# A decode kernel of two interleaved attention and feed-forward layers: all of its order tables exchanged for another set

## The chip, the cores and the metric

One core of one Trainium2 chip runs the whole program. The metric is the device time in microseconds; lower is better. The program before was timed three times.

## The reference

Four batch rows x (4 x 1 x 512) go through attention, a gated feed-forward block, the same attention and the same feed-forward block again, each with a residual:

```python
def _A_ref(x, k_cache, v_cache, wq, wo):          # k, v: 4 x 8 x 4096 x 128, bfloat16
    q = (x @ wq).reshape(B, Sq, 32, 128).transpose(0, 2, 1, 3)
    k = jnp.repeat(k_cache, 4, axis=1); v = jnp.repeat(v_cache, 4, axis=1)
    p = softmax(einsum("bhqd,bhkd->bhqk", q, k) * 128 ** -0.5)
    return einsum("bhqk,bhkd->bhqd", p, v).transpose(0, 2, 1, 3).reshape(B, Sq, 4096) @ wo
def _B_ref(x, w_gate, w_up, w_down):              # 512 x 1792, 512 x 1792, 1792 x 512
    return (sigmoid(x @ w_gate) * (x @ w_up)) @ w_down

x = x + _A_ref(layernorm(x), k_cache, v_cache, wq, wo)
x = x + _B_ref(layernorm(x), w_gate, w_up, w_down)
x = x + _A_ref(layernorm(x), k_cache, v_cache, wq, wo)
x = x + _B_ref(layernorm(x), w_gate, w_up, w_down)
```

Both layers read the same caches: 4 batches x 8 heads x (K and V) of 1 MB each, 64 MB in one layer.

## The kernel before

**Units and pairs.** A unit is one layer, one batch and one key-value head; there are 2 x 4 x 8 = 64, numbered in the order in which they run. Two neighbouring heads make a pair; the 32 pairs are numbered g = 0 to 31, and `ORDER` lists them as (layer, batch, pair of heads). Unit i belongs to pair i // 2.

**Slots.** A K or V tile of a unit fills one slot. There are 12, and when the last batch's second query product is done, the four tiles of the query weights WQ become four more (`wq_done`). `RET` names the tiles that stay in their slots from layer 0 to layer 1, 30 in all; these are loaded once, the others twice. A K slot comes free behind the last `scores` that reads it, a V slot behind the last `pv`. `LOADS` is the order of all loads on SyncE's queue: `k` and `v` are the next unit's K and V, `o` is the next tile of the output weights WO (which one, by `WO_ORDER`), `s` the next of the six halves of the gate, up and down weights (WG, WU, WD). `pump()` is called after each instruction that frees a slot, and issues loads in this order until one needs a slot and none is free. SyncE runs in order, so a load that waits for its slot holds up all behind it.

**Steps.** Step k carries the scores and softmax of pair k and the PV product of pair k - 1, unless `EARLY` lets a pair's PV run in its own step. Within a step:

- `k_turn` transposes a K tile in place on VectorE (L1164), whole or in two halves; `scores` are the products of the query with K (L1180); `smax`, `spread_max`, `softmax` find the maximum, spread it over the rows (L1240) and take the exponentials with their sum on ScalarE (L1265); `ptrans` turns the weights (L1310), and 16 small copies, shared between ScalarE (L1344) and VectorE (L1338) by `SHARE`, lay them out; `pv` multiplies with V (L1414). `PV_WIDE` repeats the columns of the moving operand to 32, 48 or 64 of which four are used. `normalise` (L1505) divides by the sums.
- `wo_mm` projects a pair's output, and where two batches or layers meet it does both at once. By `WO_ROW` it runs in column form (32 products, L1566) or in row form (16 products L1536, a copy on ScalarE L1545, four turning products L1549). `WO_AT` gives its place in the step.
- `STEP` codes four choices per step: where the next pair's K tiles are transposed (`turn_at`, `late`), whether in halves (`cut`), whether `pv` stands ahead of `spread_max` (`pv_first`), and whether a pair's two `pv` stand together (above 71). `FIRST_AT` gives the place at which the next pair's first scores are issued.
- `FILL` puts products of the identity with itself (L1199, `fill`), whose result nobody reads, on TensorE's queue at a place of a step.

```python
turn_at, pv_first, cut, late = STEP[k] % 3, STEP[k] // 3 % 2, STEP[k] // 6 % 4, STEP[k] // 24 % 3
...
pv_both, pv_late = both and STEP[k] > 71 and pv_first, both and STEP[k] > 71 and not pv_first
```

**Between the layers.** When a batch has all eight heads of layer 0, 23 pieces (`pass_steps`) carry it through the feed-forward block and the query of layer 1: `ln_a` (sums, L752), `wide` (up and gate products, L973), the inverse root by Newton steps on VectorE, `up_copy`, `gate_mul` (L996, L1001), `h_turn` (L1016), `down` (L1087), `down_add` (L1109), `ln_a` again, `q_row` (L1034), `q_out`, `q_turn`, `q_spread` (L878). `PLACES` gives each piece a step and a place. Batches 0, 1, 2 and 3 do so in this order.

**The start and the end.** The WO rows are loaded in pairs and put in order by `wo_turn` (L636, and copies L646 and L651) at the places of `WO_TURN`. The last pair's V comes in quarters (`v_parts`), its products (`pv_last`, L1441) interleave with its output projection (L1775) and with sums that give the mean (L1797, prepared by `wo_sum` at the places of `WSUM`). `AHEAD` places the first three batches' layer norm for the last feed-forward block; that block then runs for all four batches (L920, L2018) and writes the output.

**Order.** All engines run their instructions in program order; waits between engines are semaphores. Each table only moves instructions or chooses a form; none changes the result's arithmetic beyond order.

Of the kernel before, what the change touches and what calls it, by code (L numbers as in the profile page):

```python
# [20 lines left out]

ORDER = [
    (0, 0, (0,)),
    (0, 0, (3,)),
    (0, 0, (2,)),
    (0, 1, (1,)),
    (0, 0, (1,)),
    (0, 2, (0,)),
    (0, 1, (0,)),
    (1, 0, (1,)),  # L30
    (1, 0, (2,)),
    (0, 1, (3,)),
    (0, 1, (2,)),
    (1, 0, (3,)),
    (1, 0, (0,)),
    (0, 2, (2,)),
# [6 lines left out]
    (0, 3, (3,)),  # L43
    (1, 2, (3,)),
    (0, 3, (0,)),
    (0, 3, (2,)),
    (0, 3, (1,)),
    (1, 2, (1,)),
    (1, 2, (0,)),
    (1, 2, (2,)),  # L50
# [5 lines left out]

PLACES = [
    (
# [4 lines left out]
    ),  # L63
    (
# [4 lines left out]
    ),  # L69
    (  # L70
# [4 lines left out]
    ),  # L75
    (
# [4 lines left out]
    ),  # L81
]


FIRST_AT = (
# [4 lines left out]
)  # L90

LOADS = (
    "kooookokovkvkkvokokvvvkksvvkksvvksskkssk",
    "vvvkkvkvkkvvkkvkvkvkvvkvkvkvkvkvkvvkvvkk",
    "kkkvvvvkkvkvkvvkkvvkkvkkvvkvvkkkvvvkvkkv",
    "kvvvkkvkvvkkkvkkvvvvvv",
)


SHARE = (  # L100
# [4 lines left out]
)  # L105


WO_AT = (
# [4 lines left out]
)  # L113


WO_ROW = (
# [4 lines left out]
)  # L121


EARLY = (
# [4 lines left out]
)  # L129


WO_ORDER = (1, 3, 7, 2, 4, 0, 6, 5)

WO_TURN = (
# [4 lines left out]
)  # L139


PV_WIDE = (
# [4 lines left out]
)  # L147


FILL = {  # L150
# [3 lines left out]
}  # L154


WSUM = (
    (7, 8), (28, 0), (22, 5), (18, 7),
    (22, 0), (29, 7), (27, 4), (29, 7),
)  # L160


AHEAD = ((29, 2), (30, 8), (32, 4))


STEP = (
# [5 lines left out]
)  # L172


# [136 lines left out]
def bass_interleave_layers__gqa_block_cached__glu_gated_glu__decode_kernel(  # L311
# [154 lines left out]
    for kinds in LOADS:  # L466
        for kind in kinds:
            if kind == "o":
                loads.append(("wo", WO_ORDER[got["o"]]))
            elif kind == "s":  # L470
# [155 lines left out]
    def wo_turn(m, ps, key):  # L626
        assert not row_live[0]
        n, a = WO_ORDER[m // 2], m % 2
        assert f"wo{n}" in S.last_write
# [1502 lines left out]
```

## Time and profile before

| | |
|---|---|
| time, median of 3 runs | 304.89 us (302.9 to 305.69) |
| profiled execution: span, first to last instruction | 306.1 us; the page gives no other time of this execution |
| mean granted TensorE clock | 0.883 |
| busy: TensorE / VectorE / ScalarE / GpSimdE | 224.3 / 205.7 / 131.2 / 26.0 us |
| read from HBM | 116.66 MB |

In a row of the windows view stand the stretch, its length, the busy time of PE, PEld, DVE, ACT and POOL with their instruction counts, the granted TensorE clock, the DMA share and GB/s. In a timeline row stand the start, the length, the engine, the line, the operation, its output and inputs, the shape and the count; in brackets the idle time before it and what ended that.

### The profile page before, as it was taken

Reading aid. Unit: us, or ns where it says so; the run is one execution under the profiler, and the core shown is the slowest. Engines: PE = TensorE matmul, PEld = TensorE weight load, DVE = VectorE, ACT = ScalarE, POOL = GpSimd, SP = SyncE. Lnnn points to the kernel's source line nnn. Section 1 sums busy time; section 2 is a strip of 40 time slices with the busy share of each in tenths; the row PEclk is TensorE's granted clock in tenths of the full one; section 3 lists DMA queues with packets and bytes.
Section 4 is the critical chain, followed back from the end, with each engine's and each line's share of the span. In section 5 each row is a group of like instructions: output and inputs, shape, how many; then the busy total and the mean of one; then the engine's idle time right before and its main releaser. Section 6 shows DMA issues by size and latency. Waiting matters only on the chain.

```text
span 306.1 us, 11460 instructions
## 1 busy us (share of the span) xinstructions
PE 224.3 (73%) x4993; PEld 157.6 (51%) x4993; DVE 205.7 (67%) x600; ACT 131.2 (43%) x521; POOL 26.0 (9%) x107
## 2 busy tenths in 40 slices
PE   0384386864687888688886777888868688987886
PEld 0331043543464466566554554665546456556676
DVE  4755677885766368875854997566788668357743
ACT  1031243552205246564451874627772443646310
POOL 0000000000000010000001110001000000012200
PEclk9999999999579897979999857589788979599977
DMA  7999999999999979999999999999999999999900
GB/s 283 420 397 415 422 414 416 418 418 421 418 416 403 388 295 418 423 415 416 388 394 378 415 422 421 419 418 422 420 416 418 413 412 415 400 345 411 377 18 3
DMA packets 20094, 117.40 MB, mean 384 GB/s; under 512 B 1992, under 2 KB 1996, under 8 KB 7500
## 3 DMA queue, kind: packets, MB, share of 16 engines
q1 hardware_dynamic: 20044, 116.67, 93.9%
q8 instruction: 39, 0.64, 0.8%
q14 instruction: 11, 0.09, 0.1%
HBM read 116.66 MB, written 0.00 MB: 381 GB/s over the span
## 4 chain that ended last, share of the span: by engine, by line
DMA 45%; PE 30%; DVE 12%; SPq 5%; ACT 4%; issue 3%; POOL 0%; POOLq 0%; DVEq 0%; ACTq 0%
DMA slot<-in_A_v_cache_dram 22%; DMA slot<-in_A_k_cache_dram 12%; PE O_ps L1414 9%; DMA wd<-in_B_w_down_dram 6%; DVE slot L1164 6%; DMA wo<-in_A_wo_dram 5%; PE S_ps L1180 5%; ACT pT L1344 2%; SPq L550 2%; SPq L528 2%; PE M_ps L636 2%; PE O_ps L1566 2%; PE M_ps L1034 1%; PE M_ps L1087 1%; DVE wo L651 1%
## 5 line engine op out<-in xcount | busy, mean ns | idle before, releaser
L1164 DVE STREAM_TRANSPOSE slot<-slot 128x1024 f32<-128x1024 f32 (+1 forms) x61 | 100.9, 1663 | 7.0 <-DMA slot<-in_A_k_cache_dram 6.9
L1344 ACT ACTIVATE pT<-PT 32x64 bf16<-32x64 f32 x392 | 84.3, 215 | 31.9 <-PE PT L1310 26.9
L1414 PE MATMUL O_ps<-pT,slot 128*128 128x32 bf16 (+2 forms) x1888 | 65.8, 190 | 16.2 <-DMA slot<-in_A_v_cache_dram 9.6
L1414 PEld LDWEIGHTS O_ps<-pT,slot 128*128 128x128 bf16 x1888 | 59.6, 101 | 23.3 <-DMA slot<-in_A_v_cache_dram 10.6
L1180 PE MATMUL S_ps<-slot,qz 128*32 128x256 bf16 x1008 | 48.9, 329 | 12.5 <-DVE slot L1164 7.2
L1265 ACT ACTIVATE pe<-S_ps,small 128x256 bf16<-128x256 f32 x32 | 15.2, 474 | 63.3 <-DVE small L1253 63.2
L1180 PEld LDWEIGHTS S_ps<-slot,qz 128*32 128x32 bf16 x1008 | 25.3, 107 | 24.8 <-DVE slot L1164 9.2
L1279 POOL TENSOR_TENSOR small<-small 128x1 f32<-128x1 f32 x64 | 12.4, 193 | 217.6 <-ACT pe L1265 215.1
L646 ACT ACTIVATE wo<-M_ps 128x512 bf16<-128x512 f32 x14 | 8.3, 595 | 35.0 <-PE M_ps L636 35.0
L1338 DVE CAST pT<-PT 32x64 bf16<-32x64 f32 x88 | 19.4, 221 | 5.6 <-PE PT L1310 4.1
L1566 PE MATMUL O_ps<-oT,wo 128*128 128x32 bf16 x576 | 19.7, 188 | 1.1 <-issue 0.5
L636 PE MATMUL M_ps<-wo,row 64*128 64x512 bf16 x56 | 13.3, 565 | 9.1 <-DVE wo L651 5.5
L1566 PEld LDWEIGHTS O_ps<-oT,wo 128*128 128x128 bf16 x576 | 18.2, 101 | 2.1 <-DVE oT L1505 1.1
L1217 DVE TENSOR_REDUCE small<-S_ps 128x1 f32<-128x256 f32 x32 | 13.2, 413 | 8.0 <-PE S_ps L1180 7.8
L903 POOL TENSOR_TENSOR qz<-qc,norm 128x128 bf16<-128x128 bf16 x32 | 12.6, 399 | 45.5 <-ACT qc L889 45.5
L1240 PE MATMUL MS<-row_max,mask_f 128*128 128x16 bf16 x64 | 6.6, 176 | 13.1 <-DVE row_max L1223 12.6
L651 DVE CAST wo<-M_ps 128x512 bf16<-128x512 f32 x14 | 9.5, 680 | 9.6 <-PE M_ps L636 9.5
L1505 DVE TENSOR_TENSOR oT<-O_ps,rden 128x8 bf16<-128x8 f32 x31 | 4.9, 159 | 14.4 <-PE O_ps L1414 9.8
L1240 PEld LDWEIGHTS MS<-row_max,mask_f 128*128 128x128 bf16 x64 | 4.3, 107 | 19.2 <-DVE row_max L1223 17.7
L1199 PE MATMUL MS<-ident_bf 128*128 128x256 bf16 x69 | 12.2, 316 | 0.4
L1310 PE MATMUL PT<-ident_bf,pe 128*128 128x128 bf16 x64 | 10.0, 245 | 2.9 <-ACT pe L1265 2.6
L1253 DVE CUSTOM_DVE_ANT_0 row_max<-MS,small 128x16 bf16<-128x16 f32 x32 | 7.0, 217 | 7.3 <-PE MS L1240 7.1
(143 smaller groups left out, 231.1 us busy)
## 6 DMA issues: line engine op xcount, KB each, us to landing
slot<-in_A_v_cache_dram SPq DMA_DIRECT2D x49, 1024.0 KB, 12.5
slot<-in_A_k_cache_dram SPq DMA_DIRECT2D x43, 1024.0 KB, 11.3
wq<-in_A_wq_dram SPq DMA_DIRECT2D x4, 1024.0 KB, 7.8
wo<-in_A_wo_dram SPq DMA_DIRECT2D x8, 512.0 KB, 15.8
wq<-in_A_v_cache_dram SPq DMA_DIRECT2D x3, 1024.0 KB, 12.3
slot<-in_A_v_cache_dram SPq DMA_DIRECT2D x8, 256.0 KB, 13.6
wg<-in_B_w_gate_dram SPq DMA_DIRECT2D x2, 896.0 KB, 18.9
wu<-in_B_w_up_dram SPq DMA_DIRECT2D x2, 896.0 KB, 16.2
```

Source lines behind the costliest of these rows:

```text
L636: (lambda h, i, rows: lambda e: e.matmul(ps[h][:, :], lhsT=spread_w[i][rows, :], rhs=wo_sb[rows, c + i, :], start=(i == 0), stop=(i == 1), ...
L651: lambda e: e.tensor_copy(wo_sb[:, c + 1, :], ps[1][:, :]),
L903: lambda e: e.tensor_tensor(qz_sb[z][:, :, 0:4 * REP].rearrange("p i (a r) -> p i a r", r=REP), qc_sb[:, b, u:u + 2, :, :].rearrange("p u ...
L1164: dve(lambda e: e.transpose(kf, kf), writes=[f"s{st}"])
L1180: (lambda t, b2, e_, w0, s: lambda e: e.matmul(S_ps[p][32 * s:32 * s + 8 * REP, 0:2 * P], lhsT=qzf[:, w0:w0 + 8 * REP], rhs=ktv[:, :, s, : ...
L1217: lambda e: e.tensor_reduce(m, S_ps[p][:, 0:2 * P], AX.X, ALU.max),
L1265: lambda e: e.activation(to, frm, ACTF.Exp, bias=nm_sb[p], scale=exp_scale, accum_out=sm_sb[p][0],),
L1279: (lambda n: lambda e: e.tensor_tensor(sm_sb[p][n + 1], sm_sb[p][n], top(sm_sb[p][n]), ALU.subtract))(n),
L1338: (lambda dst, frm: lambda e: e.tensor_copy(dst, frm))(dst, frm),
L1344: (lambda dst, frm: lambda e: e.activation(dst, frm, ACTF.Copy))(dst, frm),
L1414: (lambda x, c, j: lambda e: e.matmul(O_ps[p][:, ul * OW:ul * OW + PV_WIDE[g]].rearrange("p (w n) -> p w n", n=REP), lhsT=vv[:, x * JG + c ...
L1566: (lambda c, r: lambda e: e.matmul(wide_out(O_ps[p], OWO + c, nb), lhsT=wo_sb[:, u * REP + r, bass.ds(2 * P * (c // 2) + c % 2, P, step=2) ...
```

## The change

Fifteen tables get other values; no line of the code and no entry of `RET` changes, so 30 tiles stay held. The new values come from a search that judges each choice by twenty runs of a model in which random waits are doubled.

- `ORDER` changes within pairs 1 to 10 and swaps pairs 23 and 24; `LOADS`, `WO_ORDER`, `WO_TURN` follow another order of loads.
- `FILL` goes from 16 places and 69 products that run (the entry at (33, 1) is never read) to 10 places and 89 products: 24 at step 5 in place of 19, none in step 6 in place of 12, 14 in step 11, 18 in step 17, and 11, 8 and 12 at the end of steps 24 and 25 and at the start of step 26.
- `WO_ROW` has 7 pairs in row form in place of 9, pair 30 among them now; `EARLY` 2 pairs in place of 4; 13 pairs have 64 PV columns in place of 9, the last pair among them.
- `PLACES`, `STEP`, `FIRST_AT`, `WO_AT`, `SHARE`, `WSUM` and `AHEAD` move the pieces of the steps. `STEP` of the last step codes the same end of the program as before.

```diff
@@ -21,16 +21,16 @@
 
 ORDER = [
     (0, 0, (0,)),
+    (0, 0, (2,)),
     (0, 0, (3,)),
-    (0, 0, (2,)),
+    (0, 2, (0,)),
+    (0, 0, (1,)),
     (0, 1, (1,)),
-    (0, 0, (1,)),
-    (0, 2, (0,)),
     (0, 1, (0,)),
+    (1, 0, (2,)),
     (1, 0, (1,)),
-    (1, 0, (2,)),
+    (0, 1, (2,)),
     (0, 1, (3,)),
-    (0, 1, (2,)),
     (1, 0, (3,)),
     (1, 0, (0,)),
     (0, 2, (2,)),
@@ -43,8 +43,8 @@
     (0, 3, (3,)),
     (1, 2, (3,)),
     (0, 3, (0,)),
+    (0, 3, (1,)),
     (0, 3, (2,)),
-    (0, 3, (1,)),
     (1, 2, (1,)),
     (1, 2, (0,)),
     (1, 2, (2,)),
@@ -56,119 +56,115 @@
 
 PLACES = [
     (
-        (2, 2), (2, 3), (2, 3), (2, 3), (2, 4), (2, 4),
-        (2, 4), (2, 4), (2, 4), (3, 2), (3, 3), (3, 4),
-        (3, 5), (3, 5), (3, 5), (3, 5), (3, 5), (3, 5),
-        (3, 5), (3, 5), (3, 5), (3, 6), (3, 6),
+        (2, 3), (2, 4), (2, 4), (2, 5), (2, 5), (2, 5), (2, 5), (2, 6), (2, 6),
+        (2, 8), (2, 8), (3, 0), (3, 1), (3, 2), (3, 2), (3, 2), (3, 2), (3, 2),
+        (3, 4), (3, 5), (3, 5), (3, 6), (3, 6),
     ),
     (
-        (2, 1), (2, 2), (2, 2), (2, 2), (2, 5), (2, 5),
-        (2, 5), (2, 5), (2, 5), (3, 1), (3, 1), (3, 2),
-        (3, 4), (3, 6), (3, 6), (3, 6), (3, 7), (3, 7),
+        (2, 1), (2, 2), (2, 2), (2, 3), (2, 4), (2, 4), (2, 6), (2, 6), (2, 6),
+        (3, 0), (3, 0), (3, 2), (3, 4), (3, 6), (3, 6), (3, 6), (3, 7), (3, 7),
         (3, 7), (3, 7), (3, 7), (3, 8), (3, 8),
     ),
     (
-        (1, 8), (2, 0), (2, 0), (2, 1), (2, 2), (2, 2),
-        (2, 2), (2, 2), (2, 2), (2, 3), (2, 4), (2, 6),
-        (2, 7), (3, 0), (3, 1), (3, 1), (3, 1), (3, 1),
-        (3, 1), (3, 2), (3, 2), (3, 6), (3, 6),
+        (1, 8), (2, 1), (2, 1), (2, 1), (2, 1), (2, 1), (2, 2), (2, 2), (2, 2),
+        (2, 5), (2, 5), (2, 6), (3, 0), (3, 0), (3, 0), (3, 1), (3, 1), (3, 1),
+        (3, 2), (3, 2), (3, 5), (3, 6), (3, 6),
     ),
     (
-        (1, 8), (2, 1), (2, 1), (2, 1), (2, 1), (2, 1),
-        (2, 2), (2, 2), (2, 2), (2, 3), (2, 4), (2, 6),
-        (2, 8), (3, 1), (3, 2), (3, 3), (3, 3), (3, 5),
-        (3, 5), (3, 5), (3, 5), (3, 6), (3, 6),
+        (1, 8), (2, 1), (2, 1), (2, 1), (2, 1), (2, 1), (2, 1), (2, 1), (2, 2),
+        (2, 3), (2, 3), (2, 6), (2, 8), (2, 8), (2, 8), (2, 8), (2, 8), (2, 8),
+        (3, 1), (3, 4), (3, 4), (3, 5), (3, 5),
     ),
 ]
 
 
 FIRST_AT = (
-    7, 7, 6, 7, 5, 6, 1, 3,
-    8, 7, 1, 3, 1, 0, 4, 8,
-    2, 7, 5, 2, 7, 1, 7, 7,
-    0, 5, 2, 7, 8, 8, 3,
+    6, 8, 8, 2, 4, 7, 6, 1,
+    5, 2, 0, 6, 1, 8, 8, 5,
+    7, 2, 4, 2, 7, 1, 8, 7,
+    0, 3, 7, 4, 2, 1, 6,
 )
 
 LOADS = (
-    "kooookokovkvkkvokokvvvkksvvkksvvksskkssk",
-    "vvvkkvkvkkvvkkvkvkvkvvkvkvkvkvkvkvvkvvkk",
-    "kkkvvvvkkvkvkvvkkvvkkvkkvvkvvkkkvvvkvkkv",
-    "kvvvkkvkvvkkkvkkvvvvvv",
+    "kookoookkkvokkvvkovovkvvkvksvkvksssskksk",
+    "vvkvvkvkkvkkvkkvvkvkvvkkvkvvkvkvvkkvvkkv",
+    "vkkvkkkvvvvkvvkvkkvvkvkkkkkvvvvkkvkvvkkk",
+    "vkvvvvkkkvvkkvvvkkvvvv",
 )
 
 
 SHARE = (
-    1, 0, 1, 2, 2, 0, 2, 1,
-    0, 0, 1, 0, 1, 2, 0, 0,
-    0, 0, 0, 0, 0, 1, 0, 2,
-    1, 0, 0, 2, 1, 6, 2,
+    1, 0, 1, 0, 1, 0, 0, 1,
+    0, 1, 0, 1, 1, 2, 0, 0,
+    0, 1, 0, 1, 0, 1, 0, 1,
+    1, 0, 0, 1, 1, 6, 2,
 )
 
 
 WO_AT = (
-    0, 1, 3, 1, 2, 1, 1, 1,
-    2, 2, 1, 1, 0, 0, 0, 0,
-    3, 1, 0, 3, 1, 1, 2, 2,
-    0, 2, 3, 2, 0, 1, 0, 0,
+    3, 1, 0, 2, 1, 0, 3, 2,
+    0, 3, 0, 1, 2, 1, 2, 0,
+    1, 1, 0, 3, 1, 0, 0, 0,
+    0, 1, 2, 0, 1, 1, 0, 0,
 )
 
 
 WO_ROW = (
     0, 0, 0, 0, 0, 0, 0, 0,
-    2, 0, 0, 2, 1, 0, 0, 2,
-    0, 0, 0, 2, 0, 0, 1, 0,
-    0, 0, 0, 0, 1, 2, 0, 2,
+    0, 0, 0, 0, 0, 0, 0, 1,
+    0, 0, 0, 2, 0, 0, 0, 0,
+    0, 0, 0, 2, 1, 2, 1, 1,
 )
 
 
 EARLY = (
-    1, 0, 0, 1, 1, 0, 0, 0,
+    0, 0, 0, 0, 1, 0, 0, 0,
     0, 0, 0, 0, 0, 1, 0, 0,
     0, 0, 0, 0, 0, 0, 0, 0,
     0, 0, 0, 0, 0, 0, 0, 0,
 )
 
 
-WO_ORDER = (1, 3, 7, 2, 4, 0, 6, 5)
+WO_ORDER = (
+    4, 5, 1, 0, 7, 6, 3, 2,
+)
 
 WO_TURN = (
-    (-1, 0), (-1, 0), (-1, 0), (-1, 0),
-    (-1, 0), (0, 4), (0, 7), (4, 2),
-    (0, 4), (3, 2), (0, 0), (0, 5),
-    (1, 4), (1, 4), (3, 1), (2, 5),
+    (-1, 0), (-1, 0), (1, 4), (0, 3), (0, 4), (-1, 0), (-1, 0), (-1, 0),
+    (2, 7), (0, 3), (0, 6), (1, 6), (3, 1), (4, 5), (2, 2), (3, 8),
 )
 
 
 PV_WIDE = (
-    32, 48, 48, 48, 32, 48, 48, 32,
-    64, 48, 64, 64, 48, 48, 32, 32,
-    32, 48, 64, 32, 32, 64, 64, 48,
-    32, 32, 64, 48, 64, 48, 64, 48,
+    64, 48, 32, 64, 48, 64, 32, 64,
+    32, 48, 48, 32, 32, 48, 48, 64,
+    32, 64, 64, 64, 64, 32, 48, 64,
+    64, 48, 32, 32, 32, 48, 64, 64,
 )
 
 
 FILL = {
-    (3, 8): 1, (4, 6): 6, (5, 1): 6, (5, 2): 5, (5, 8): 8, (6, 0): 4,
-    (6, 4): 6, (6, 7): 2, (8, 2): 8, (11, 1): 8, (11, 5): 1, (12, 1): 5,
-    (18, 7): 3, (22, 2): 4, (25, 5): 2, (33, 1): 1,
+    (0, 8): 1, (5, 2): 11, (5, 8): 13, (8, 8): 1, (11, 0): 14, (17, 0): 7,
+    (17, 2): 11, (24, 8): 11, (25, 8): 8, (26, 1): 12,
 }
 
 
 WSUM = (
-    (7, 8), (28, 0), (22, 5), (18, 7),
-    (22, 0), (29, 7), (27, 4), (29, 7),
+    (21, 7), (25, 4), (10, 1), (14, 8), (21, 4), (23, 7), (24, 4), (11, 7),
 )
 
 
-AHEAD = ((29, 2), (30, 8), (32, 4))
+AHEAD = (
+    (27, 8), (30, 2), (31, 7),
+)
 
 
 STEP = (
-    36, 18, 22, 0, 63, 12, 25, 82,
-    12, 7, 12, 6, 6, 15, 13, 108,
-    24, 108, 42, 27, 41, 102, 68, 27,
-    71, 124, 3, 38, 71, 44, 6, 4,
-    10,
+    6, 139, 36, 82, 124, 65, 5, 59,
+    10, 96, 34, 0, 96, 4, 74, 12,
+    104, 30, 58, 27, 35, 78, 140, 39,
+    67, 76, 27, 54, 33, 42, 97, 33,
+    40,
 )
```

## The prediction

> **What bounds the kernel now.** I read the page first: the span, the clock and the DMA by slices.
>
> ```profile
> span 306.1 us, 11460 instructions
> PEclk9999999999579897979999857589788979599977
> DMA  7999999999999979999999999999999999999900
> GB/s 283 420 397 415 422 414 416 418 418 421 418 416 403 388 295 418 423 415 416 388 394 378 415 422 421 419 418 422 420 416 418 413 412 415 400 345 411 377 18 3
> HBM read 116.66 MB, written 0.00 MB: 381 GB/s over the span
> ```
>
> Each slice is 7.65 us. The loads keep the DMA engines full from the first slice to slice 38, at 415 to 422 GB/s where nothing disturbs them. At 420 GB/s, 116.66 MB take 277.8 us, so some 28 us of the span are not that: the start, three soft places (slices 14 and 15, 20 to 22, 35 to 38), and two empty slices at the end. The next view is the busy time by stages, cut at these places; its last column is GB/s, the one before it the DMA share, the one before that the granted clock.
>
> ```profile
> 5.00:90.00 85.00, 52.66 (x921) 31.05 (x922) 59.08 (x140) 24.65 (x86) 4.44 (x17) 0.94 1.02 416
> 90.00:115.00 25.00, 20.29 (x428) 13.24 (x425) 13.31 (x58) 10.07 (x39) 2.26 (x9) 0.93 0.94 365
> 140.00:170.00 30.00, 23.46 (x602) 17.08 (x599) 18.53 (x71) 13.38 (x55) 2.27 (x9) 1.00 0.99 391
> 170.00:240.00 70.00, 55.43 (x1300) 40.63 (x1298) 53.59 (x133) 40.52 (x172) 6.69 (x27) 0.78 1.01 420
> 265.00:280.00 15.00, 13.16 (x320) 9.58 (x316) 7.63 (x39) 7.96 (x33) 2.26 (x9) 0.87 0.97 363
> 290.80:306.10 15.30, 11.34 (x355) 10.72 (x351) 6.12 (x37) 1.64 (x6) 0.39 (x2) 0.78 0.03 10
> ```
>
> Against 420 GB/s the place at 90 to 115 loses 25 x (1 - 365/420) = 3.3 us (**A**), that at 140 to 170 loses 2.1 us (**B**), that at 265 to 280 loses 2.0 us (**C**). After 290.8 nothing is loaded, and 15.3 us of arithmetic follow. From 170 to 240 the DMA loses nothing although the clock is 0.78: TensorE is covered there.
>
> Why A, B and C: a load is issued when a slot comes free, so I walked through the tables, once with the old and once with the new, and wrote down for every load which instruction frees its slot and how many bytes stand ahead. A, B and C are the feed-forward and query steps of batches 0, 1 and 3 between the layers. SyncE's own timeline shows its issues there (second number: until the last issue of the merged row):
>
> ```profile
> 87.97 15.69 SPq L550 DMA_DIRECT2D slot<-in_A_v_cache_dram  x4
> 108.25 4.16 SPq L550 DMA_DIRECT2D slot<-in_A_k_cache_dram  x4
> 142.97 8.91 SPq L550 DMA_DIRECT2D slot<-in_A_v_cache_dram  x5
> 248.88 14.02 SPq L550 DMA_DIRECT2D slot<-in_A_v_cache_dram  x6
> 267.04 0.33 SPq L550 DMA_DIRECT2D slot<-in_A_k_cache_dram  x1
> 269.10 0.33 SPq L550 DMA_DIRECT2D wq<-in_A_k_cache_dram  x1
> ```
>
> At A the fourth V load goes out at 103.3 and the next load, K18, only at 108.25: 4.9 us in which 1 MB (2.5 us) is all that was added. At C the sixth goes out at 262.6, K62 at 267.04, then WQ's four slots come free at 269.10.
>
> **The change, part by part.** The held units (RET) are the same, so are the 116.66 MB, the number of K transposes and the code. What moves is order. In the walk the least distance between the last input that a freeing instruction can depend on and the moment at which the queue would be empty is 5.0 us (two loads) with both sets of tables; it occurs four times with the old, eight with the new. So the new order has no more room; I price the three places and the end.
>
> *A.* The fourth V load is V13, freed by pv of unit 10; K18 is freed by pv of unit 11, with both tables. What stands before them:
>
> ```profile
> 94.03 1.04 PE L1199 MATMUL MS<-ident_bf 128*128 128x256 bf16 x8
> 98.80 1.02 PE L1087 MATMUL M_ps<-wd,qT 128*1 128x256 bf16 x14 [0.90 <-DMA wd<-in_B_w_down_dram]
> 100.85 1.25 PE L1199 MATMUL MS<-ident_bf 128*128 128x256 bf16 x6
> 107.25 0.96 PE L1414 MATMUL O_ps<-pT,slot 128*128 128x48 bf16 x32
> ```
>
> The first half of the down product waits for WD's landing, at the same place in LOADS with both tables. The old order then has six fills (1.25 us) and down_add before pv 10. The new one does both halves at once, with no fill behind them; its 13 fills stand ahead of the down product, 13 x 0.13 (1.04/8, full clock) to 13 x 0.21 (1.25/6, half clock) = 1.7 to 2.7 us. They follow scores of unit 12, which ended at about 94.0, and so end by 96.7, inside the wait for WD until 98.8; uncovered, they would cost those 1.7 to 2.7. Scores of unit 13 move behind the down product, so V12 goes out some 4 us later, while V10 and V11 are still being moved. Gain between 0 and 1.7 us (1.25, and 0.4 for the four fills of step 6 that go); I take **-0.8**.
>
> *B.* V22 changes places with K27, which puts it 1 MB = 2.5 us later, and scores of unit 24, which frees a slot, moves from before pv 20 to after pv 21:
>
> ```profile
> 137.69 0.64 PE L1180 MATMUL S_ps<-slot,qz 128*32 128x256 bf16 x16
> 139.78 1.14 PE L1414 MATMUL O_ps<-pT,slot 128*128 128x64 bf16 x32 [0.28 <-DMA slot<-in_A_v_cache_dram]
> 146.19 1.12 PE L1414 MATMUL O_ps<-pT,slot 128*128 128x64 bf16 x32
> ```
>
> The first is scores 24, the second pv 21, the third pv 22. Scores 24 would end 3.2 us later (139.78 + 1.14 + 0.64 against 138.33), and pv 22 up to 2.5 us if V22 was only just there. The queue at this place is thin (the stage runs at 391). Bounds 0 (the loads ahead cover it) and 2.0 (as much again as the stage loses now); **+0.7**.
>
> *C.* In the new order 8 fills stand ahead of batch 3's first sum (step 25), 12 ahead of its up product (step 26), and 11 at the end of step 24.
>
> ```profile
> 245.63 1.03 PE L1414 MATMUL O_ps<-pT,slot 128*128 128x32 bf16 x32 [1.86 <-DMA slot<-in_A_v_cache_dram]
> 248.05 2.31 DVE L1164 STREAM_TRANSPOSE slot<-slot 128x2048 f32<-128x2048 f32 x1 [0.28 <-DMA slot<-in_A_k_cache_dram]
> 250.47 0.38 PE L752 MATMUL M_ps<-xT,small 128*128 128x4 f32 x2 [0.62 <-DVE xT L1587]
> 251.44 2.31 DVE L1164 STREAM_TRANSPOSE slot<-slot 128x2048 f32<-128x2048 f32 x1
> 251.52 0.57 PE L973 MATMUL M_ps<-wu,xc_bf 128*1 128x448 bf16 x8
> 259.95 1.19 PE L1566 MATMUL O_ps<-oT,wo 128*128 128x32 bf16 x32
> 265.12 1.89 PE L1414 MATMUL O_ps<-pT,slot 128*128 128x64 bf16 x32
> 270.63 0.28 PE L878 MATMUL M_ps<-qT,ident_bf 128*32 128x32 bf16 x16 [0.28 <-DVE qT L1075]
> ```
>
> The 11 lie in the wait for V49 (1.86 us until 245.63): nothing; uncovered 1.4 to 2.3. The 20 cost 2.6 to 4.2 us on PE's queue. Ahead of the sum 0.6 us is PE's wait, and between the up product at 251.52 and the end of the transpose at 253.75, behind which the inverse root is queued on VectorE, lie 2.2 us, of which the sum of squares uses about half. Left on the path: 0.8 to 2.4. Behind the fills are queued the up and gate products, pv 50 (which frees V53's slot, and now stands behind the gate product too) and pv 51. The other way, an output projection (1.19 us) that stood between down product and query moves behind the query's first half. Net -0.4 to +1.2; **+0.5**. From 245.63, where PE waits for V49, to the end the chain is arithmetic: the loads end at 290.8 and the last pair's PV starts at 293.93 (below), so what the DMA loses here is hidden up to some 3 us.
>
> *The end.* The output projection of pair 30 changes from column form to row form, the last PV from 48 to 64 columns, and the three batches' inverse roots move a step earlier, off VectorE's end.
>
> ```profile
> 288.06 0.61 PE L1536 MATMUL O_ps<-wo,oT 128*2 128x256 bf16 x16
> 289.06 0.38 ACT L1545 ACTIVATE row<-O_ps 128x256 f32<-128x256 f32 x1
> 289.77 0.61 PE L1549 MATMUL O_ps<-sel,row 128*128 128x4 f32 x4
> 293.10 0.99 PE L1566 MATMUL O_ps<-oT,wo 128*128 128x32 bf16 x27 [0.54 <-issue]
> 293.93 1.44 PE L1441 MATMUL O_ps<-slot,slot 128*128 128x48 bf16 x32
> ```
>
> Row form: 0.61 + 0.38 + 0.61 = 1.6 us and its waits; column form: 0.99 for 27 of 32 with 0.54 ahead. Even, or 0.3 gained. A group of 32 at 64 columns took 1.14 (full clock, 139.78) to 1.89 (half, 265.12) against 1.44 here: up to +0.45 for each of two groups. Bounds -0.3 and +1.0; **+0.2**.
>
> *The rest*, at nothing: the early order (WO tiles, first pairs), covered by a full queue at 416 GB/s until 90, and otherwise some 3.7 us (the first steps need the fourth WO tile and K1, 1.5 MB later); 69 fills become 89 and wide PV 9 pairs become 13, 0.2 us a group, both under the DMA between A and C; fewer early pairs and another split of the copies likewise.
>
> Sum: -0.8 + 0.7 + 0.5 + 0.2 = +0.6, so 306.7 for the profiled execution. The page gives no time beside its span of 306.1, which lies 1.2 above the median of 304.89; I carry the +0.6 to the median: **305.5 us**. With all low bounds -2.4, with all high ones +4.2.
>
> **The rivals.** *Half of the stalls go* (faster). The order is smoother than my walk sees and A, B and C lose half of 7.4 us: 304.9 - 3.7 = 301.2. For it: the fills that go at A stand on the path; against: no more room between loads. 0.10.
>
> *The fills hold the clock* (faster).
>
> ```profile
> 248.50:258.80 10.30, 8.38 (x215) 5.65 (x203) 9.13 (x23) 5.63 (x21) 0.39 (x2) 1.00 1.01 418
> 258.80:269.00 10.20, 10.13 (x139) 5.98 (x136) 3.77 (x21) 5.30 (x21) 0.39 (x2) 0.50 0.97 389
> ```
>
> Batch 3's steps ran 10.2 us at half clock, PE busy throughout; at full clock at most 5 of it go. With 31 fills ahead the clock may stay up: half of that, 2.5, and the fills cost about 0.8 less: 305.5 - 3.3 = 302.2. Against: the clock fell after 10.3 us in which PE was busy for 8.38, so more busy time ahead need not help. The Trainium skill, "TensorE: Matmul & The Clock Gate" (Part 1, The HAM clock gate), says that the clock halves after an idle window of some 3.4 us and that activity lifts it. The trace disagrees at 258.8, where no such idle stretch stands ahead. 0.10.
>
> *The fills delay the last query* (slower): at C all 20 run at half clock and nothing hides them, 4.2 us on the chain from 245.63 to the end; it decides as soon as the up product starts after 254. With A and B cancelling: 304.9 + 4.2 + 0.2 = 309.3. For it: nothing waits for these fills but what follows them, and the chain behind has no DMA cover. 0.20.
>
> **How the numbers follow.** My forecast 0.60, the rivals 0.10, 0.10 and 0.20. One per cent, 3 us, is about what a measurement of this kernel can tell; the forecast's own range, 302.5 to 309.1, is within it but for its upper end. The range 301.2 to 309.4 reaches to all three rivals and leaves out about half of the first and the third, 0.15 to 0.2 in all. Faster by over 1% (below 301.8): 0.10 from the first and half of the second, 0.15. Slower (above 307.9): the third and 0.06 of the forecast's upper end, 0.26. Within: 0.59.
>
> **What would show it.** Right: A at 370 to 385 GB/s, B below 391, 12 fills just ahead of the up product and that product 0.8 to 2.4 us later behind V49's landing than the 5.9 of now; loads ending near 291; a tail of 15 us. Wrong: A or B at 410 (first rival); full clock through batch 3's steps (second); the last query's end over 28 us after V49's landing, where it is now 25 (third); or a stall before 90, where I put none.

## The result, and the profile after

I call the two kernels *before* and *after*. Over 20 executions each, the kernel after has a median of 306.19 us (303.95 to 311.01) and the kernel before one of 304.48 us (301.25 to 306.77). The ratio is 1.0065 with the interval [1.004, 1.0089]: 2.0 us slower, 1.2 to 2.7. Medians in this document are over all executions; ratios and intervals leave out the few that were disturbed, and so are not the quotients of the medians. The forecast was 305.5, and its likeliest case, a change of less than 1%, is what came.

These three lines are from the page of after: span, granted clock and GB/s by slices of 7.6 us. V49 is the V tile of unit 49, K27 the K tile of unit 27, and so on. A line number (L1176) names the same operation with another number in another kernel, because the tables ahead of the code take up different numbers of lines; go by the tile names and shapes.

```profile
span 304.6 us, 11503 instructions
PEclk9999999966775999687958999999995999999597
GB/s 278 422 397 419 417 422 410 416 421 419 419 407 412 394 342 419 420 421 374 363 421 362 425 417 415 420 417 424 417 423 417 400 422 396 412 396 418 385 38 3
```

This execution took 306.45 us, 1.8 more than its span. The profiled execution of before that the prediction rests on has the longer span, 306.1, and so some 307.9 us: it lies above all 20 of its own kernel. I therefore profiled the kernel before once more (span 304.0, time 305.74) and read every term against both traces. Two single traces are not two medians.

Busy time by stages, after. The last three columns are the granted clock, the DMA share and GB/s.

```profile
5.00:90.00 85.00, 52.12 (x907) 31.80 (x907) 56.12 (x130) 28.05 (x100) 4.86 (x19) 0.90 1.02 416
90.00:115.00 25.00, 21.83 (x448) 14.46 (x449) 12.48 (x48) 11.56 (x47) 1.89 (x7) 0.86 0.97 383
140.00:170.00 30.00, 24.34 (x547) 16.14 (x536) 18.14 (x69) 12.78 (x50) 2.28 (x9) 0.80 0.97 379
240.00:270.00 30.00, 25.91 (x612) 19.13 (x608) 21.01 (x69) 16.11 (x66) 2.29 (x10) 1.00 1.00 407
270.00:290.00 20.00, 16.86 (x397) 12.73 (x398) 11.88 (x43) 8.24 (x34) 3.80 (x15) 0.83 1.00 395
```

The same stages in the second profile of before:

```profile
5.00:90.00 85.00, 52.24 (x908) 30.85 (x909) 58.82 (x140) 24.59 (x86) 4.44 (x17) 0.70 1.02 417
90.00:115.00 25.00, 20.92 (x445) 14.14 (x442) 14.63 (x59) 10.75 (x43) 2.26 (x9) 1.00 0.96 379
140.00:170.00 30.00, 23.48 (x601) 17.12 (x602) 20.75 (x76) 15.49 (x64) 2.26 (x9) 1.00 1.00 408
240.00:270.00 30.00, 24.27 (x504) 16.33 (x508) 18.56 (x57) 13.60 (x55) 2.26 (x9) 0.77 0.99 399
270.00:290.00 20.00, 15.73 (x431) 12.80 (x424) 13.57 (x52) 10.02 (x39) 3.83 (x15) 1.00 0.96 366
```

A (90 to 115) is hardly better, B (140 to 170) is worse, and the clock has changed places: it is full in batch 3's steps (240 to 270), where it was 0.77, and down at the end (270 to 290), where it was full. Up to 90 the loads run as before (416 GB/s, against 416 and 417).

TensorE's timeline of after, at A, C and the end:

```profile
91.49 0.92 PE L969 MATMUL M_ps<-wu,xc_bf 128*1 128x448 bf16 x8 [2.82 <-DMA wu<-in_B_w_up_dram]
95.52 1.04 PE L1176 MATMUL S_ps<-slot,qz 128*32 128x256 bf16 x16
96.50 2.10 PE L1195 MATMUL MS<-ident_bf 128*128 128x256 bf16 x13
98.43 0.51 PE L1012 MATMUL M_ps<-ident_bf,row 128*128 128x2 bf16 x8
99.22 0.93 PE L1083 MATMUL M_ps<-wd,qT 128*1 128x256 bf16 x28 [0.28 <-DVE qT L1022]
...
245.13 1.13 PE L1410 MATMUL O_ps<-pT,slot 128*128 128x64 bf16 x32 [1.38 <-DMA slot<-in_A_v_cache_dram]
251.21 1.48 PE L1195 MATMUL MS<-ident_bf 128*128 128x256 bf16 x12
252.63 0.57 PE L969 MATMUL M_ps<-wu,xc_bf 128*1 128x448 bf16 x8
266.81 0.28 PE L874 MATMUL M_ps<-qT,ident_bf 128*32 128x32 bf16 x16 [0.28 <-DVE qT L1071]
...
285.00 1.04 PE L1176 MATMUL S_ps<-wq,qz 128*32 128x256 bf16 x16
286.15 1.02 PE L1532 MATMUL O_ps<-wo,oT 128*2 128x256 bf16 x16
291.16 0.61 PE L1532 MATMUL O_ps<-wo,oT 128*1 128x256 bf16 x16
292.26 0.63 PE L1545 MATMUL O_ps<-sel,row 128*128 128x2 f32 x4 [0.49 <-ACT row L1541]
292.75 1.09 PE L1437 MATMUL O_ps<-slot,slot 128*128 128x64 bf16 x32
```

The same points in the second profile of before:

```profile
243.39 1.03 PE L1333 MATMUL O_ps<-pT,slot 128*128 128x32 bf16 x32 [1.85 <-DMA slot<-in_A_v_cache_dram]
268.53 0.28 PE L797 MATMUL M_ps<-qT,ident_bf 128*32 128x32 bf16 x16 [0.28 <-DVE qT L994]
286.44 0.67 PE L1099 MATMUL S_ps<-wq,qz 128*32 128x256 bf16 x16
287.21 0.61 PE L1455 MATMUL O_ps<-wo,oT 128*2 128x256 bf16 x16
291.42 1.23 PE L1485 MATMUL O_ps<-oT,wo 128*128 128x32 bf16 x32
292.49 0.96 PE L1360 MATMUL O_ps<-slot,slot 128*128 128x48 bf16 x32
```

From V49's landing to the last query's end (`q_spread`) after takes 266.81 - 245.13 = 21.7 us, where before took 25.0 and 25.1. From there to the last pair's PV it takes 292.75 - 266.81 = 25.9, where before took 23.3 and 24.0. From that PV to the end of the span it takes 11.9, where before took 12.2 and 11.5. So the last query gave 3.3 to 3.5 us, and the steps behind it gave 2.0 to 2.6 of these back. V49 itself landed at 245.13 in after and at 245.63 and 243.39 in the two profiles of before: up to there two executions of one kernel differ by 2.2 us, more than the whole change.

### The profile page after: what moved, and what is told of

It reads as the page before. It is cut to its first block, busy times and chain, and to the rows that moved or that the text cites. A ratio compares the mean times of both kernels' runs of the same rounds, so it can differ in the third digit from the quotient of the medians.

```text
span 304.6 us, 11503 instructions
## 1 busy us (share of the span) xinstructions
PE 224.1 (74%) x5013; PEld 158.8 (52%) x5013; DVE 202.0 (66%) x581; ACT 135.0 (44%) x537; POOL 26.1 (9%) x107
## 4 chain that ended last, share of the span: by engine, by line
DMA 41%; PE 34%; DVE 15%; ACT 5%; issue 2%; SPq 2%; POOL 0%; POOLq 0%; DVEq 0%
DMA slot<-in_A_v_cache_dram 17%; DMA slot<-in_A_k_cache_dram 13%; PE O_ps L1410 10%; DVE slot L1160 8%; DMA wo<-in_A_wo_dram 6%; PE S_ps L1176 5%; DMA wu<-in_B_w_up_dram 5%; ACT pT L1340 3%; PE M_ps L1030 2%; PE M_ps L632 2%; PE MS L1195 2%; PE M_ps L1083 1%; PE O_ps L1562 1%; DVE small L1213 1%; PE PT L1306 1%
## 5 line engine op out<-in xcount | busy, mean ns | idle before, releaser
L1340 ACT ACTIVATE pT<-PT 32x64 bf16<-32x64 f32 x408 | 87.8, 215 | 33.0 <-PE PT L1306 27.7
L1160 DVE STREAM_TRANSPOSE slot<-slot 128x1024 f32<-128x1024 f32 (+1 forms) x58 | 98.3, 1704 | 5.9 <-DMA slot<-in_A_k_cache_dram 5.9
L1410 PE MATMUL O_ps<-pT,slot 128*128 128x64 bf16 (+2 forms) x1920 | 68.3, 191 | 16.7 <-DMA slot<-in_A_v_cache_dram 9.2
L1410 PEld LDWEIGHTS O_ps<-pT,slot 128*128 128x128 bf16 x1920 | 62.2, 101 | 26.1 <-ACT pT L1340 9.0
L1176 PE MATMUL S_ps<-slot,qz 128*32 128x256 bf16 x992 | 45.0, 311 | 18.0 <-DVE slot L1160 14.7
L1176 PEld LDWEIGHTS S_ps<-slot,qz 128*32 128x32 bf16 x992 | 23.1, 102 | 30.4 <-DVE slot L1160 18.2
L1562 PE MATMUL O_ps<-oT,wo 128*128 128x32 bf16 x576 | 19.1, 185 | 0.3 <-DVE oT L1501 0.3
L642 ACT ACTIVATE wo<-M_ps 128x512 bf16<-128x512 f32 x13 | 7.7, 596 | 24.8 <-PE M_ps L632 24.8
L1334 DVE CAST pT<-PT 32x64 bf16<-32x64 f32 x72 | 15.8, 219 | 3.1 <-PE PT L1306 2.0
L632 PE MATMUL M_ps<-wo,row 64*128 64x512 bf16 x52 | 11.8, 543 | 6.0 <-ACT wo L642 3.2
L1501 DVE TENSOR_TENSOR oT<-O_ps,rden 128x8 bf16<-128x8 f32 x31 | 4.9, 159 | 15.5 <-PE O_ps L1410 11.5
L1030 PE MATMUL M_ps<-wq,xc_bf 128*1 128x512 bf16 x128 | 11.2, 437 | 1.1 <-DVE xc_bf L761 0.9
```

The source lines that it names most:

```text
L632: (lambda h, i, rows: lambda e: e.matmul(ps[h][:, :], lhsT=spread_w[i][rows, :], rhs=wo_sb[rows, c + i, :], start=(i == 0), stop=(i == 1), ...
L1030: (lambda k, st: lambda e: e.matmul(M_ps[h][32 * st:32 * st + 1, :], lhsT=xc_bf[:, k, 0:1], rhs=wv[:, k, h, :, st, :], start=(k == 0), sto ...
L1160: dve(lambda e: e.transpose(kf, kf), writes=[f"s{st}"])
L1176: (lambda t, b2, e_, w0, s: lambda e: e.matmul(S_ps[p][32 * s:32 * s + 8 * REP, 0:2 * P], lhsT=qzf[:, w0:w0 + 8 * REP], rhs=ktv[:, :, s, : ...
L1334: (lambda dst, frm: lambda e: e.tensor_copy(dst, frm))(dst, frm),
L1340: (lambda dst, frm: lambda e: e.activation(dst, frm, ACTF.Copy))(dst, frm),
```

## The experiments

Each mix takes the new tables for some steps and the old ones for the rest. **Early** is steps 0 to 10 (batch 0's pieces, the WO turns, the loads up to K26), **middle** steps 11 to 22 (batches 1 and 2), **last query** steps 23 to 27 (batch 3 and its 31 fills), **end** steps 28 to 32 with `AHEAD` and the order of the last loads. `WSUM`, the places of the copies for the weight sums, is new in every mix that has the new last query or the new end. The last four columns are from the windows view of each kernel's one profile: GB/s of A and B, and the granted clock of batch 3's steps and of the end. A row of before closes each block of kernels that ran together on one chip, and gives its median there. Each diff below is a cut and shows a part of the tables that the mix changes.

| new parts | median, us | ratio to before | A, GB/s | B, GB/s | clock 240-270 | clock 270-290 |
|---|---|---|---|---|---|---|
| early | 306.58 | 1.0111 [1.0066, 1.0156] | 381 | 402 | 0.66 | 1.00 |
| middle | 307.83 | 1.0139 [1.0093, 1.0185] | 385 | 370 | 0.66 | 1.00 |
| last query | 303.83 | 1.0021 [0.9989, 1.0054] | 387 | 399 | 1.00 | 1.00 |
| end | 304.16 | 1.0020 [0.9987, 1.0053] | 365 | 405 | 0.89 | 0.74 |
| *before: 303.82* | | | | | | |
| all but middle | 306.59 | 1.0070 [1.0031, 1.0109] | 386 | 410 | 1.00 | 0.66 |
| all, and 5 fills at step 12 | 306.79 | 1.0045 [1.0006, 1.0084] | 383 | 390 | 1.00 | 0.91 |
| all but the 31 late fills | 306.62 | 1.0070 [1.0042, 1.0098] | 384 | 376 | 0.77 | 0.83 |
| none (before, once) | 305.74 | | 379 | 408 | 0.77 | 1.00 |
| *before: 304.40* | | | | | | |
| all but end | 305.34 | 1.0057 [1.002, 1.0094] | 384 | 374 | 1.00 | 0.91 |
| early and last query | 304.40 | 1.0008 [0.9976, 1.0041] | 383 | 392 | 0.97 | 0.91 |
| none, and the 31 late fills | 304.89 | 1.0022 [0.9981, 1.0062] | 388 | 408 | 0.94 | 0.93 |
| *before: 304.40* | | | | | | |
| all, but V22 and scores 24 as before | 305.02 | 1.0038 [1.0003, 1.0074] | 385 | 404 | 1.00 | 0.83 |
| *before: 304.22* | | | | | | |
| all (after) | 306.19 | 1.0065 [1.004, 1.0089] | 383 | 379 | 1.00 | 0.83 |
| none (the first profile) | | | 365 | 391 | 0.77 | 1.00 |

**Which part costs?** Four kernels with one new part each.

Early:

```diff
 FILL = {
-    (3, 8): 1, (4, 6): 6, (5, 1): 6, (5, 2): 5, (5, 8): 8, (6, 0): 4, (6, 4): 6, (6, 7): 2, (8, 2): 8,
+    (0, 8): 1, (5, 2): 11, (5, 8): 13, (8, 8): 1,
...
```

> New tables for steps 0 to 10 (order of pairs 0 to 10, loads up to K26, batch 0's pieces between the layers, all WO turns), old tables from step 11 on. Sum theory (the prediction's term A): 0.8 us faster than the kernel before, and in the trace the stage 90 to 115 at 370 to 390 GB/s where the kernel before has 365. Last-query theory (the fills at steps 24 to 26 carry the whole loss) and end theory (steps 28 on carry it): no change to 0.5 us either way. Interaction theory (only the whole set loses): within 0.5 us.

Middle:

```diff
 FILL = {
...
-    (11, 1): 8, (11, 5): 1, (12, 1): 5, (18, 7): 3, (22, 2): 4,
+    (11, 0): 14, (17, 0): 7, (17, 2): 11,
...
```

> New tables for steps 11 to 22 only (V22 behind K27, scores of unit 24 behind pv 21, batches 1 and 2 between the layers, 14 and 18 fills), old ones elsewhere. Sum theory (term B): 0.7 us slower (0 to 2.0), stage 140 to 170 below the 391 GB/s of the kernel before. Last-query and end theories: no change. Interaction theory: within 0.5 us.

Last query:

```diff
 FILL = {
...
-    (25, 5): 2,
+    (24, 8): 11, (25, 8): 8, (26, 1): 12,
...
```

> New tables for steps 23 to 27 only (pairs 23 and 24 swapped, 11, 8 and 12 fills, batch 3 between the layers, V50 behind K55; the copies for the weight sums at their new places too), old ones elsewhere. Sum theory (term C): 0.5 us slower (-0.4 to 1.2). Last-query theory: 2 to 4 us slower. Clock theory (the fills hold the clock up): faster by 2 us or more, and full clock from 245 to 270. End theory: no change.

End:

```diff
-AHEAD = ((29, 2), (30, 8), (32, 4))
+AHEAD = ((27, 8), (30, 2), (31, 7))
 LOADS, the last nine
-    "vkkvvvvvv"
+    "vvvkkvvvv"
...
```

> New tables for steps 28 to 32 only (pair 30 projected in row form, 64 columns in the last PV, the three batches' layer norm earlier, K62 and K63 loaded behind V58 and V59), old ones elsewhere. Sum theory (the end's term): 0.2 us slower (-0.3 to 1.0). End theory: 1.5 to 2 us slower, the whole of what the changed kernel loses. Last-query theory: no change.

Early alone costs 1.1% and middle alone 1.4%; the last query and the end alone cost nothing that can be told. Added up, these ratios give 1.029, and the whole change gives 1.0065: the parts do not add. The losses of early and middle, some 3.4 and 4.2 us, lie outside every expectation above; six executions each stand behind them. The next row is batch 3's stage in the profile of the kernel with only early new. Its tables for batch 3's steps are those of before:

```profile
240.00:270.00 30.00, 25.91 (x505) 16.89 (x493) 18.62 (x57) 13.85 (x55) 1.77 (x8) 0.66 0.98 384
```

In the profiles of these two kernels some 20 of the 30 us there ran at half clock, against some 14 in before, though nothing was changed at that place. That is not where most of their time goes: from V49's landing to `q_spread` both take 25.7 us, 0.6 more than before.

**Is it the middle?** Everything new except the middle:

```diff
 FILL = {
...
-    (11, 0): 14, (17, 0): 7, (17, 2): 11,
+    (11, 1): 8, (11, 5): 1, (12, 1): 5, (18, 7): 3, (22, 2): 4,
...
```

> The changed kernel with the old tables for steps 11 to 22. The first runs' loads fell back by 3.1 to 3.6 us between K26 and V32 with the new middle and by 1.2 to 2.2 with the old one. Middle theory (the change's loss is there): 1.8 us faster than the changed kernel, so 0 to 0.3 us from the kernel before or faster, and the stage 140 to 170 at 400 GB/s in place of 379. Sum theory with its 0.7: 305.5. Seam theory (a mixed set loses, as the run with the new early tables did by 3.3): 306.5 or more.

B is back at 410 GB/s, and the time stays at 1.0070. The middle's loss is in the trace, but by time it can't be seen: [1.0031, 1.0109] without the new middle and [1.004, 1.0089] with it leave room for some 0.5% either way.

**Would fills bring back the clock at B?** The old 5 fills of step 12, added to the kernel after:

```diff
 FILL = {
...
+    (12, 1): 5,
...
```

> The changed kernel with five more fills at the place at which the kernel before has them (step 12, ahead of batch 1's first sum). Clock theory for the middle (the new set has no fill there, and its clock fell to half from 152 to 162): full clock from 150 to 165, 1 us of the loss gone, 305.2. Order theory (V22 behind K27 and the scores behind the PV cost it): no change, or 0.5 us slower for the fills.

B: 390 GB/s at a clock of 0.83, against 379 at 0.80. The full clock that the clock theory expected did not come, and the ratio of 1.0045 can't be told from that of after. So this run could not test the clock itself; that B stayed low fits the order theory.

**The late fills, taken away and added alone.** First all new tables without the 31, then, in a later block, the kernel before with only these 31:

```diff
 FILL = {
...
-    (24, 8): 11, (25, 8): 8, (26, 1): 12,
...
```

> The changed kernel without its 31 fills at the ends of steps 24 and 25 and the start of step 26. Clock theory (they hold the clock up for batch 3's pieces; the clock was full from 240 to 280 in both runs that had them and fell to half there in three of the four that had not): half clock somewhere from 245 to 270 and 1.5 to 3 us slower. The prediction's term C (the fills cost 0.8 to 2.4 us of path): 0.5 to 2 us faster.

```diff
 FILL = {
...
+    (24, 8): 11, (25, 8): 8, (26, 1): 12,
...
```

> The kernel before with the 31 fills of the changed kernel at the ends of steps 24 and 25 and the start of step 26, nothing else. Clock theory: full clock from 245 to 270, where both its profiles had 14 us at half, V49's landing to WQ's release 22 to 23 us in place of 26, and 0.5 to 2 us faster. Prediction's term C alone (fills on the path): 0.8 to 2.4 us slower.

Batch 3's stage without them:

```profile
240.00:270.00 30.00, 25.67 (x566) 18.24 (x562) 20.11 (x64) 15.30 (x62) 2.28 (x9) 0.77 0.99 398
```

V49's landing and `q_spread` in the same profile:

```profile
245.01 1.89 PE L1318 MATMUL O_ps<-pT,slot 128*128 128x64 bf16 x32 [1.26 <-DMA slot<-in_A_v_cache_dram]
267.68 0.28 PE L782 MATMUL M_ps<-qT,ident_bf 128*32 128x32 bf16 x16 [0.28 <-DVE qT L979]
```

The same stage, and three points of TensorE's timeline, in the kernel before with them:

```profile
240.00:270.00 30.00, 25.36 (x611) 18.58 (x607) 20.72 (x68) 14.90 (x59) 2.27 (x9) 0.94 1.00 406
```

```profile
242.88 1.02 PE L1336 MATMUL O_ps<-pT,slot 128*128 128x32 bf16 x32 [2.09 <-DMA slot<-in_A_v_cache_dram]
265.69 0.28 PE L800 MATMUL M_ps<-qT,ident_bf 128*32 128x32 bf16 x16 [0.28 <-DVE qT L997]
290.23 1.15 PE L1363 MATMUL O_ps<-slot,slot 128*128 128x48 bf16 x32
```

With the fills the clock of this stage is 0.94 to 1.00 in eight profiles of eight; without them it is 0.66 to 0.89 in six of six. Added to the kernel before, V49 to `q_spread` takes 22.8 us (25.0 and 25.1 without). But the same old steps without any fill took 21.4 in the profile of the kernel with only the end new (265.73 below, less 244.34), where the clock of the stage was 0.89:

```profile
240.00:270.00 30.00, 24.39 (x594) 17.32 (x592) 21.53 (x72) 15.55 (x63) 2.28 (x9) 0.89 1.01 413
244.34 1.04 PE L1332 MATMUL O_ps<-pT,slot 128*128 128x32 bf16 x32 [1.63 <-DMA slot<-in_A_v_cache_dram]
```

In this profile the old order had that time without any fill, while the clock stayed up. And the new steps without the fills take 22.7 us at a clock of 0.77 (the profile of all but the 31), against 21.6 to 21.7 with them in five profiles: of the 3.3 to 3.5 us that the last query gave, about 1.0 goes with the fills, and the rest came with the other new tables at the same low clock.

By time neither run moves: 1.0022 for the kernel before with them, and 1.0070 without them against 1.0065 for after. The first interval leaves 0.6 us faster to 1.9 slower: the clock theory's 0.5 to 2 us are all but excluded, term C's 0.8 to 2.4 are not. Its 1.5 to 3 us for the second did not come either. Nor is the clock higher over the whole program: over their timed executions on this chip its mean is 0.85 with the fills and 0.86 for the kernel before. So the fills hold the clock in one stage, and no gain from it can be measured here.

**The kernel before, profiled again:**

No line differs.

> The kernel before once more, for a second profile of it. Its span of 306.1 in the first profile would be 1.5 us above the slowest of its 20 unprofiled runs if the time is the span and 1.8 us, as in the changed kernel's runs; so a span of 300 to 304 is expected, and full clock for a larger part of 245 to 270.

Its rows stand above. The span of 304.0 is at the upper end of what was expected, and the clock of 240 to 270 is 0.77 again, not higher. (The first profile lies 1.1 us above the slowest of the 20, 307.9 against 306.77, not 1.5.) B alone moves between 391 and 408 GB/s from one execution of the same kernel to the next, and A between 365 and 379.

**Does the end take the gain back?** Everything new but the end, and early with the last query:

```diff
-AHEAD = ((27, 8), (30, 2), (31, 7))
+AHEAD = ((29, 2), (30, 8), (32, 4))
 WO_ROW, pair 30
-    1
+    0
...
```

> The changed kernel with the old tables for steps 28 to 32. End theory, second form (the new end loses the clock: in all five profiles with the new end some of 270 to 293 ran at half clock and WQ's release to the last PV took 26.2 to 29.2 us; in the five with the old end none did and it took 24.8 to 26.3): full clock from 270 to 293, that stretch near 25.5, and 1.5 to 2.5 us faster than the changed kernel. Middle theory alone (the loads' 1.7 us between K26 and V32): no change. Sum theory: 0.2 us faster.

The second is the first with the old middle as well:

```diff
 FILL = {
...
-    (11, 0): 14, (17, 0): 7, (17, 2): 11,
+    (11, 1): 8, (11, 5): 1, (12, 1): 5, (18, 7): 3, (22, 2): 4,
...
```

> The new tables for steps 0 to 10 and 23 to 27, the old ones for steps 11 to 22 and 28 to 32: of each part the tables whose profiles were the better ones. If the parts add up as in the profiles (loads 1.7 us earlier than in the changed kernel, the last query at full clock, the end at full clock): a span of 300 to 301.5 and 302 to 303.3 us, 1 us or more below the kernel before. Seam theory (a mixed set loses what its search had joined): 305 or more.

The end in the profile of the kernel with only the end new, TensorE's timeline:

```profile
265.73 0.28 PE L796 MATMUL M_ps<-qT,ident_bf 128*32 128x32 bf16 x16 [0.28 <-DVE qT L993]
285.20 1.04 PE L1098 MATMUL S_ps<-wq,qz 128*32 128x256 bf16 x16
290.32 0.61 PE L1454 MATMUL O_ps<-wo,oT 128*1 128x256 bf16 x16
291.91 1.09 PE L1359 MATMUL O_ps<-slot,slot 128*128 128x64 bf16 x32
```

From `q_spread` to the last pair's PV it takes 26.2 us, although its early, middle and last query are old: the 25.9 of after goes for the most part with the new end. Six kernels have the new end; in five profiles of them this stretch is 25.9 to 27.7 us, in the sixth (with the 5 fills at step 12) 24.8. With the old end it is 23.3 to 24.8 in seven profiles of eight, and 26.0 in that of early with the last query. Not all of it is the end's: with the old end the four profiles without the late fills have 23.3 to 24.0 and the four with them 24.5 to 26.0, so behind a stage with the fills this stretch is longer with either end. With the fills the ranges of the two ends overlap.

By time the old end brings after from 1.0065 to 1.0057, which can't be told apart; the 1.5 to 2.5 us that the end theory expected did not come. Early with the last query alone is even with the kernel before (1.0008), not 1 us below it as expected, although early alone cost 1.1%. The middle on top of it has 1.0057, the end on top of it 1.0070, both together 1.0065: about half a per cent more each, but the intervals of the first two overlap that of 1.0008, [0.9976, 1.0041], and the last two ran in other blocks.

**B, its cause undone.** The kernel after with V22 ahead of K27 and scores 24 ahead of pv 20, as before:

```diff
 FIRST_AT, entry 11
-    6
+    3
 LOADS, loads 61 to 68
-    "vvkkvkvv"
+    "vvkvkkvv"
```

> The changed kernel with two entries as before: V22 is loaded ahead of K27, and the scores of unit 24 stand ahead of pv 20 again. Order theory (these two, the prediction's term B, are what puts the loads back between K26 and V32): the loads fall back there by 2.0 to 2.5 us in place of 3.1 to 3.7, and 0.7 us faster than the changed kernel at most, less if the end costs it anyway. Clock theory (half clock from 152 to 162 is the cause): still 3.1 us or more wherever the clock falls there, and no change of the time.

The stage at B and SyncE's issues there in this kernel:

```profile
140.00:170.00 30.00, 24.78 (x596) 17.04 (x596) 19.91 (x77) 15.29 (x60) 2.28 (x9) 0.83 1.01 404
```

```profile
132.61 0.33 SPq L463 DMA_DIRECT2D slot<-in_A_v_cache_dram  x1
136.46 0.33 SPq L463 DMA_DIRECT2D slot<-in_A_k_cache_dram  x1
141.77 8.87 SPq L463 DMA_DIRECT2D slot<-in_A_v_cache_dram  x5
```

SyncE's issues in after, and then in the first profile of before:

```profile
107.37 2.83 SPq L546 DMA_DIRECT2D slot<-in_A_k_cache_dram  x2
132.88 0.33 SPq L546 DMA_DIRECT2D slot<-in_A_k_cache_dram  x1
140.74 10.85 SPq L546 DMA_DIRECT2D slot<-in_A_v_cache_dram  x6
```

```profile
134.75 0.33 SPq L550 DMA_DIRECT2D slot<-in_A_v_cache_dram  x1
138.38 0.33 SPq L550 DMA_DIRECT2D slot<-in_A_k_cache_dram  x1
```

In after K27 takes the first free slot at 132.88, and V22 gets the one that scores 24 frees, at 140.74. For 7.9 us no load goes out. With both put back the longest pause is 5.3 us (136.46 to 141.77) and B runs at 404 GB/s, at a clock of 0.83, where the kernel with the 5 fills had the new order, the same clock and 390: the place in the queue was the cause, not the clock. V22's place and that of scores 24 were put back together, so their shares stay untold. The ratio of this kernel, 1.0038 [1.0003, 1.0074], is the lowest of those with all four new parts, but its interval overlaps that of after.

No kernel here beats the kernel before: early with the last query, the last query alone, the end alone and the kernel before with the late fills can't be told from it, and all others are slower.

## Why the prediction was right, and where it was not

The time came out 0.7 us from the forecast and inside its range, but by luck. The change is +2.0 us where +0.6 was forecast, and the two times lie closer because the 304.89 that the forecast started from, of three executions, was 0.4 above the median of twenty. And no term of the sum had its size: one had the wrong sign, two were too small, one was too large, and the error of C, the largest, cancels those of the other three.

**A, -0.8 forecast.** The stage runs at 381 to 386 GB/s in eight profiles with the new early part (mean 383.6) and at 365 to 388 in six with the old one (mean 378.2): 25 x 5.4/420 = 0.3 us gained, and that is less than the old order varies. The four of the six whose clock was full in this stage have 379 to 388, so against them nothing is gained. K18 goes out at 107.37, not 108.25, but in the second profile of before it goes out at 107.37 too. The step that failed is that the 13 fills end by 96.7. They begin at 96.50, behind scores that end there and not at 94.0, because the up product, which starts as early as in before, is at half clock:

```profile
91.34 0.56 PE L973 MATMUL M_ps<-wu,xc_bf 128*1 128x448 bf16 x8 [0.43 <-DMA wu<-in_B_w_up_dram]
```

This is the row of before; after has 0.92 us from 91.49. The fills take 2.10 us. WD's second half landed at 98.5 (issued at 79.14, 19.4 us to its landing), so most of them was still covered, as forecast; but `h_turn` and its copy, which the forecast did not count, stand behind the fills, and the down product waits for VectorE until 99.22. About 0.7 us of what I called covered was on the path.

**B, +0.7 forecast, bounds 0 to 2.0.** The mechanism was right and the term too small. The stage ran at 370 to 390 GB/s in five profiles with the new order of V22 (mean 378) and at 391 to 410 in eight with the old one (mean 402): 30 x 24/420 = 1.7 us. My price came from how late pv 22 would be. It is not late (146.38, where before has 146.19); what is late is the queue, 7.9 us without an issue.

**C, +0.5 forecast.** The sign was wrong. The step that the fills make the up product later held: it starts 7.5 us behind V49's landing instead of 5.9, 1.6 later, and 12 fills stand just ahead of it (251.21). But from there to `q_spread` it takes 14.2 us, not 19.1. In sum -3.3 to -3.5 us to `q_spread`, more than the second rival asked for. Its mechanism, a clock that the fills hold up, is there, but accounts for about 1.0 of it, by one profile: without the fills the new steps took 22.7 us. The term had priced the fills and one output projection, and put the rest of the new order of these steps at nothing.

**The end, +0.2 forecast.** The tail behind the last pair's PV was as forecast, within 0.4 us. I had looked no further than that: the loss of 2.0 to 2.6 us lies ahead of it, between `q_spread` and the last PV. Two pieces of it can be read off. The last two scores ran, in part or whole, at half clock in all six kernels with the new end (1.04 us for 16; with the old end 0.64 to 0.67 where nothing interrupted them), and in after `wo_mm` behind them took 1.02, not 0.61. And the row form of pair 30 takes 1.59 us from its first product to the last PV, where column form took 1.07 in the second profile of before: I had priced it from an execution in which the column form held a 0.54 us pause. New in these steps are some narrower PV products, some whole in place of halved transposes, and later K62 and K63; which of them lowers the clock was not tried alone, and part of the longer stretch came behind the late fills with the old end too.

**The rivals.** Half of the stalls didn't go: A moved by 0.3 us and B got worse. The fills did not delay the last query: it ended 21.7 us behind V49's landing, not 28. The fills held the clock: full clock through batch 3's steps, which the prediction had named as a sign of being wrong, is what after's profile shows. But the 2.5 us did not come.

**What stays open.** By the stages the change is worth -0.3 at A, +1.7 at B, -3.3 to -3.5 at C and +2.0 to 2.6 behind it, -0.1 to 0.7 in sum; by time it costs 1.2 to 2.7. Where the rest goes is not shown. Both profiled executions of before (some 307.9, and 305.74) are slower than its median, and had 0.77 in batch 3's steps. Executions of before with a higher clock are faster: of the 82 that stand behind the ratios of the mixes, the 22 with a mean granted clock below 0.845 have a median of 305.3 us, the others 303.7. The old steps took 21.4 us without fills in the one profile in which their clock stayed up, so C's gain over a usual execution of before is probably smaller than these profiles show. That would also fit the two runs with and without fills, but no fast execution of before itself was profiled, so it isn't shown. Nor is it shown why early alone loses 1.1% and loses nothing beside the new last query; the two were timed on different chips.

## What to carry to other kernels

A load queue that is limited by slots is judged by its longest pause between issues, not by whether the next consumer is late: one load moved one place, with the scores that free its slot moved behind a PV, cost 1.7 us of DMA time. How much of that reached the time of the program is not shown. A stretch that a profile shows shortened by 3 us has gained nothing until the stretch behind it has been compared too, and medians of many executions decide, since here two traces of one kernel differ by 2.1 us, as much as the change. When parts of a change are tried alone, try them in pairs as well: here the parts' losses came to over four times that of the whole.

## What the hardware showed that I had not expected

TensorE's granted clock takes two levels in short windows: read in after from 270 to 295 by half microseconds it is 1.00 up to 281.5, 0.50 from 282 to 288.5 and 1.00 from 289. And it falls where TensorE is busy: it was 0.50 from 282 to 288, although PE had been busy for 4.68 of the 6.00 us before, at a clock of 0.99:

```profile
276.00:282.00 6.00, 4.68 (x127) 3.75 (x127) 3.45 (x10) 1.40 (x6) 1.10 (x5) 0.99 1.02 422
282.00:288.00 6.00, 5.49 (x102) 3.58 (x99) 4.95 (x14) 2.62 (x11) 1.96 (x7) 0.50 1.01 393
```

The Trainium skill, "TensorE: Matmul & The Clock Gate" (Part 1, The HAM clock gate), gives in its table two levels and an idle window of some 3.4 us as what halves the clock. The levels agree with the trace; the condition does not, since all idle time in those 6 us comes to 1.3. And 31 products whose result nobody reads kept the half clock out of one stage, most of it or all (0.94 to 1.00, against 0.66 to 0.89 without them), without a change of the time that could be measured.
